# The first batch's weight conversion on fixed engine orders, one weight item per slot, low bits joined by an or on VectorE

## The chip, the cores and the metric

The kernel runs on one core of a Trainium2 chip. The metric is the device time of one execution in microseconds (us), as the median of several runs. A profile is one further execution, taken with the hardware profiler; it gives every instruction's start and length on five engines: TensorE (PE, with its weight loads as PEld), VectorE (DVE), ScalarE (ACT), GpSimd (POOL) and SyncE (SP, which here only issues the DMAs).

## The reference, cut to what matters

Three layers follow each other: an attention with 32 landmarks per head, a two-matrix layer with an exponential activation, and a maxout layer of three matrices followed by an output matrix. The weights are float64 in memory.

```
A = softmax(q @ mean(k)); Bm = softmax(mean(q) @ mean(k)); C = softmax(mean(q) @ k)
Z = start(Bm); six times: Z = 2 * Z - Z @ Bm @ Z
x = A @ Z @ C @ v                       # 8 batches of 576 tokens, 512 wide
h = x @ w_in                            # 512 -> 2048
g = where(h > 0, h, exp(min(h, 0)) - 1)
y = g @ w_out                           # 2048 -> 512
out = max(y @ w1, y @ w2, y @ w3) @ w_out2
```

## The kernel before, in words

Matrix products run as three passes in a reduced format (a high and a low part of each operand), so every operand is split: ScalarE casts the high part, and VectorE or GpSimd subtracts it from the value to get the low part (`split`, L105).

The attention of a batch ends in matrices that are folded into `w_in` (`w_step`, L645 and L650 write the folded weights `wp`). The second layer then runs in **slots**. A slot is one block of 128 hidden columns for half of a batch's tokens (288): six matmuls into `ph` (`h_mm`, L677); ScalarE's two activations of `eh` (L681, L682); VectorE's combination of them (`h_post`, L687, "eh" below); the split of the result into `gt`; and twelve matmuls `x<-gt,wo` (`x_mm`, L709), which follow three slots later (`LAG`). The first batch has slots 0 to 31, and the attention of the second batch is spread over them (`SECOND_SLOTS`): its sums stand at slots 3 to 6, its six Newton steps n0 to n5 at slots 20 to 25. A Newton step is `banks<-rr,rd` on TensorE (L237), then `rd` (L560) and `rr` (L613) on VectorE and a copy of `rr` (L611) on ScalarE. `ph` has two buffers: the matmuls of slot t need the eh of slot t-2 to be done.

In the first batch the float64 weights arrive as 32-bit words and are converted on the chip. An **item** is a block of 128 rows and 512 columns; there are 32, items 0 to 31, in the order of `PAIRS` (i: `w_in`, o: `w_out`). `widen` puts two instructions on ScalarE: a Prelu that makes a float of the upper word (L121), and a Copy that brings the three next bits of the lower word to an integer (L124). `narrow` shifts the float's bits left by three on VectorE (L130) and adds the integer on GpSimd (L133). An item of `w_out` is then split into `wo`. Items land in places that later hold other tiles; an item is loaded when the earlier holder of its place has been narrowed. By that plan items 28 and 29 follow items 24 and 25 in their places, item 30 follows item 28, and item 31 follows item 29.

Before the first slot, VectorE and ScalarE run in the written order `ORDER` ("c" narrows a pair of items, "w" widens one, the capitals are steps of the first batch's attention). From slot 0 a scheduler sets the order of all engines by priority; from slot 20 (`FIXED`) TensorE and VectorE follow the written order. ScalarE, GpSimd and SyncE follow the scheduler. Each engine works strictly through its own list, and so does SyncE with the DMAs.

Of the kernel before, what the change touches and what calls it, by code (L numbers as in the profile page):

```python
# [9 lines left out]
F32 = mybir.dt.float32  # L10
# [9 lines left out]
def landmark_attention_mlp_maxout_kernel(  # L20
# [13 lines left out]
    nc = tc.nc  # L34
# [16 lines left out]
    FPN = 512 // P  # L51
    LAG = 3

    FIXED = 20
    RA = 3

    AHEAD2 = 5
# [9 lines left out]
    PAIR_SLOTS = [0, 0, 0, 1, 1, 4, 6, 8, 9, 11, 12, 14, 15, 18, 20, 22]  # L67


    ORDER = "BBBBBBwVwBcBVVwVVwBcVVBAwBAwcBAwcBAAwBAcBAwBAAWAwcwcc"  # L70


    PAIR_LOW = [0, 0, 1, 0, 0, 1, 0, 1, 0, 0, 1, 0, 0, 0, 1, 0]
    G_LOW = [
        [0, 1, 1, 0, 0, 1, 0, 0, 1, 0, 1, 1, 0, 0, 1, 0],
        [0, 0, 0, 1, 0, 1, 1, 1, 0, 0, 0, 1, 0, 0, 0, 1],
    ]
    SOFT_SUB = [[1, 1], [1, 1]]
    SOFT_MUL = [[1, 0], [0, 0]]
    scale = 1.0 / math.sqrt(D)  # L80
# [20 lines left out]
    def split(src, hi, lo, on_dve=False):  # L101

        nc.scalar.copy(hi, src)  # L103
        eng = nc.vector if on_dve else nc.gpsimd
        eng.tensor_tensor(out=lo, in0=src, in1=hi.bitcast(F32), op=ALU.subtract)  # L105
# [6 lines left out]
            in_=src.rearrange("(f p) c -> p f c", p=P),  # L112
        )

    def widen(words, f):
# [10 lines left out]
    def narrow(words, f):  # L126


        u = f.bitcast(U32)
        nc.vector.tensor_scalar(  # L130
            out=u, in0=u, scalar1=3, scalar2=None, op0=ALU.logical_shift_left
        )
        nc.gpsimd.tensor_tensor(out=u, in0=u, in1=words[:, :, 0], op=ALU.add)  # L133
        yield

    class Conversions:
# [3 lines left out]
        def __init__(self, items, depth):  # L140
            self.items, self.depth = items, depth
            self.words, self.f = {}, {}
            self.done = -1
            self.run = self.steps()

        def fetch(self):
# [3 lines left out]
                if t is not None:  # L150
                    self.words[n] = t

        def widen(self, n):
            if n < len(self.items) and n not in self.f:
                if n not in self.words:
                    self.fetch()
                if n not in self.words:
                    return
                self.f[n] = self.items[n][1]()
                widen(self.words[n], self.f[n])  # L160

        def steps(self):
            for n in range(0, len(self.items), 2):
                both = range(n, min(n + 2, len(self.items)))
                for m in both:
                    self.widen(m)
                for _ in zip(*[narrow(self.words[m], self.f[m]) for m in both]):
                    yield
                for m in both:
                    outs = self.items[m][2]  # L170
                    if outs is not None:
                        split(self.f[m], *outs(), PAIR_LOW[n // 2])
                    self.done = m
                    self.fetch()
                for m in both:
                    if m + 2 < len(self.items) and self.items[m + 2][2] is None:
                        self.widen(m + 2)
                if self.items[n][2] is not None:
                    yield

        def upto(self, n):

            n = min(n, len(self.items))
            while self.done < n - 1:
                next(self.run)

    manual = ExitStack()
    manual.enter_context(
# [505 lines left out]
    def x_mm(b, half, f):  # L694
# [3 lines left out]
        first = f % (KF // 2) == 0 if parts else f == 0  # L698
        last = f % (KF // 2) == KF // 2 - 1 if parts else f == KF - 1
        if b == 0:  # L700
            conv.upto(index["out", f] + 1)
# [520 lines left out]

    def fits(n, p):
        if p[0] == "wp":
            return n in EARLY
        return n // 2 <= index["out", 2 * p[1]] // 2

    def plan_places():
# [47 lines left out]
    conv = Conversions(items, DEPTH)  # L1276

    def w_both(n):
        conv.upto(index["in", n * KD + KD - 1] + 1)
        w_step(0, n)  # L1280

    for g, nm in ((0, "q"), (0, "k"), (1, "q"), (1, "k")):
        load_qk(0, g, nm)
    load_v(0)
    for _ in range(NF):
        conv.fetch()
    streams = {
        "B": [
# [30 lines left out]
            streams[token].pop(0)()  # L1319
    assert not any(streams.values())  # L1320
    spare[0] = -1
    conv.upto(G)
    manual.close()


    seq = [(0, half, p * KF // 2 + f) for p in range(2) for half in range(2) for f in range(KF // 2)]
# [4 lines left out]
    def at(t, fn, *args):  # L1331
        plan[t].append((fn, args))

    load_att(1)
    load_v(1)

    def after_post(stp):


# [3 lines left out]

        return go

    for n, t in enumerate(PAIR_SLOTS):
        at(t, conv.upto, 2 * n + 2)
    for n in range(1, NCH):
        tw = (0, FPN, KF, KF + FPN)[n]
        at(tw - (2 if n == 1 else 3), w_both, n)  # L1350
    for b in range(1, B):
        t0 = (b - 1) * NSL
        if b > 1:
            at(t0 - (12 if b == 2 else 13), load_att, b)
            at(t0, load_v, b)
        for nm, stp in att_steps(b):
            if b > 1:
                at(t0 + (THIRD_SLOTS.get(nm) if b == 2 and nm in THIRD_SLOTS else STEP_SLOTS[nm]), stp)
            else:
                at(SECOND_SLOTS[nm], after_post(stp))  # L1360
        for n in range(NCH):
            at(t0 + NSL + (W_SLOTS if b > 1 else SECOND_W)[n], w_step, b, n, True)
    plain = [(i, p) for p in range(NP) for i in range(2)]
# [13 lines left out]
    manual = ExitStack()  # L1377
    for t, sl in enumerate(seq):
        if t == FIXED:
            manual.enter_context(tc.manual_schedule(engines={mybir.EngineType.PE}))  # L1380
        if t == FIXED:
            vector = ExitStack()
            vector.enter_context(tc.manual_schedule(engines={mybir.EngineType.DVE}))
        h_mm(*sl)
        late = [fn(*args) for fn, args in plan[t]]
        h_post(*sl)
        for fn in late:
            if callable(fn):
                fn()
        for parts in behind[t]:  # L1390
            next(parts, None)
        if t >= LAG:
# [132 lines left out]
```

## Time and profile before

| what | value |
|---|---|
| three runs | 1355.29, 1357.17, 1357.25 us; median 1357.17 |
| profiled execution | 1356.48 us, of which its span is 1354.7 us |
| TensorE busy | 1306.1 us (96% of the span) |
| VectorE, ScalarE, GpSimd busy | 836.6, 678.5, 690.4 us |

The 1.8 us between the span and the time of the profiled execution lie around it. A busy share is a mean over stages: in the first tenth of the span TensorE waits often, and behind that it hardly does. So the page's 96% says where little can be gained, and the stretches of the first 140 us have to be read one by one.

### The profile page before, as it was taken

The page shows a single profiled execution, that of the slowest core. Times are in us where ns is not written, and L with a number is a line of the kernel's source. Part 1 is how long each engine was busy: PE and PEld are TensorE (multiplying, and loading weights), DVE is VectorE, ACT ScalarE, POOL GpSimd, SP SyncE. Part 2 cuts the span into 40 slices and gives each one's busy share as a digit, 9 for nine tenths or more (in the row PEclk, how much of TensorE's full clock was granted, in tenths as well). Part 3 has the DMA queues.
Part 4 walks back from the last instruction along what each step waited for, and adds up shares of the span by engine and source line. Part 5 has one row for each costly group of instructions (what it writes and reads, how often), then busy time and mean ns, then how long its engine had stood idle before and what let it go on. Part 6 is the DMA issues. An engine that isn't in the chain of part 4 may idle for free.

```text
span 1354.7 us, 28499 instructions
## 1 busy us (share of the span) xinstructions
PE 1306.1 (96%) x11144; PEld 1231.5 (91%) x11144; DVE 836.6 (62%) x1601; ACT 678.5 (50%) x1576; POOL 690.4 (51%) x702
## 2 busy tenths in 40 slices
PE   4688999999999999999999999999999999999998
PEld 2477889899899998998999999999999999999998
DVE  6885745546537546455464456776677667668873
ACT  4884555656656656656566662222223223235451
POOL 2781433444435425435346456666666666665543
PEclk8588999999999999999999999999999999999999
DMA  9635104124214233142116233221322122278962
GB/s 359 224 110 167 41 19 146 64 82 149 100 41 138 104 113 97 65 166 74 66 65 189 65 120 109 86 98 55 114 86 86 56 103 97 81 286 319 310 230 78
DMA packets 102376, 168.04 MB, mean 124 GB/s; under 512 B 5985, under 2 KB 57825, under 8 KB 102241
## 3 DMA queue, kind: packets, MB, share of 16 engines
q1 hardware_dynamic: 102240, 166.22, 36.1%
q8 instruction: 87, 1.43, 0.4%
q14 instruction: 49, 0.39, 0.1%
HBM read 107.22 MB, written 58.98 MB: 123 GB/s over the span
## 4 chain that ended last, share of the span: by engine, by line
PE 89%; DMA 3%; ACT 3%; DVE 2%; issue 1%; POOL 1%; SPq 0%; DVEq 0%; ACTq 0%; POOLq 0%
PE p L1063 30%; PE x L709 28%; PE ph L677 14%; PE p L1140 10%; PE banks L237 7%; DMA words<-in_moe_w_out_dram 2%; DMA kT<-in_k_dram 1%; ACT words L124 1%; DMA raw<-w2s 0%; ACT gt L103 0%; DVE tt L765 0%; DVE eh L687 0%; DVE gt L105 0%; DMA words<-in_moe_w_in_dram 0%; ACT wp L645 0%
## 5 line engine op out<-in xcount | busy, mean ns | idle before, releaser
L709 PE MATMUL x<-gt,wo 128*128 128x288 f32 x3072 | 470.6, 303 | 4.8 <-DVE gt L105 1.4
L709 PEld LDWEIGHTS x<-gt,wo 128*128 128x128 f32 x3072 | 425.2, 190 | 45.2 <-issue 26.1
L1063 PE MATMUL p<-xo,w 128*128 128x256 f32 x3402 | 410.4, 283 | 1.0 <-DVE xo L737 1.0
L1063 PEld LDWEIGHTS p<-xo,w 128*128 128x128 f32 x3402 | 408.6, 191 | 2.8 <-ACT xo L879 1.5
L105 POOL TENSOR_TENSOR gt<-eh,gt 128x288 fp32r<-128x288 f32 x243 | 198.9, 820 | 338.2 <-ACT gt L103 306.2
L677 PE MATMUL ph<-ah,wp 128*128 128x288 f32 x1024 | 251.5, 300 | 10.0 <-DVE eh L687 4.3
L687 DVE SCALAR_TENSOR_TENSOR eh<-eh,ph 128x288 f32<-128x288 f32 x256 | 114.4, 447 | 157.3 <-ACT eh L682 113.8
L918 POOL TENSOR_TENSOR u<-s,v 128x512 f32<-128x512 f32 x99 | 132.3, 1336 | 144.9 <-DVE v L916 144.9
L677 PEld LDWEIGHTS ph<-ah,wp 128*128 128x128 f32 x1024 | 182.1, 192 | 17.6 <-DVE eh L687 7.7
L103 ACT CAST gt<-eh 128x288 fp32r<-128x288 f32 x256 | 110.4, 432 | 108.3 <-DVE eh L687 108.1
L681 ACT ACTIVATE eh<-ph 128x288 f32<-128x288 f32 x256 | 104.5, 410 | 116.4 <-PE ph L677 91.2
L907 ACT COPY s<-p 128x512 f32<-128x512 f32 x99 | 57.9, 585 | 198.9 <-PE p L1063 172.2
L677 PE MATMUL ph<-al,wp 128*128 128x288 f32 x512 | 153.7, 300 | 2.1 <-POOL al L105 2.1
L1140 PE MATMUL p<-wo,ho 128*128 128x256 f32 x1134 | 133.2, 280 | 0.0
L1140 PEld LDWEIGHTS p<-wo,ho 128*128 128x128 f32 x1134 | 133.1, 188 | 0.0
L682 ACT ACTIVATE eh<-eh 128x288 f32<-128x288 f32 x256 | 113.8, 446 | 5.1
L677 PEld LDWEIGHTS ph<-al,wp 128*128 128x128 f32 x512 | 98.3, 192 | 2.5 <-POOL al L105 2.5
L931 DVE TENSOR_TENSOR t<-p,u 128x512 f32<-128x512 f32 x81 | 55.8, 689 | 72.1 <-POOL u L918 69.5
L1130 DVE TENSOR_TENSOR ho<-hf,ho 128x768 fp32r<-128x768 f32 x54 | 73.6, 1390 | 13.6 <-ACT ho L1128 12.8
L1070 DVE TENSOR_TENSOR t<-t 128x1024 f32<-128x1024 f32 x54 | 70.6, 1307 | 6.4 <-POOL t L921 0.4
L921 POOL TENSOR_TENSOR t<-u,s 128x256 f32<-128x256 f32 x81 | 67.1, 829 | 5.4
L133 POOL TENSOR_TENSOR wf<-wf,words 128x512 uint32<-128x512 uint32 x40 | 54.9, 1381 | 28.9 <-DVE wf L130 22.9
(164 smaller groups left out, 1391.8 us busy)
## 6 DMA issues: line engine op xcount, KB each, us to landing
hf<-hs SPq DMA_DIRECT2D x63, 384.0 KB, 4.5
hs<-t SPq DMA_DIRECT2D x27, 512.0 KB, 3.0
xs<-xo SPq DMA_DIRECT2D x36, 288.0 KB, 3.3
hs<-s SPq DMA_DIRECT2D x27, 384.0 KB, 3.4
qT<-in_q_dram SPq DMA_DIRECT2D x16, 576.0 KB, 6.3
kT<-in_k_dram SPq DMA_DIRECT2D x16, 576.0 KB, 7.5
words<-in_moe_w_dram SPq DMA_DIRECT2D x9, 1024.0 KB, 5.1
xf<-xs SPq DMA_DIRECT2D x9, 1024.0 KB, 5.0
```

Source lines behind the costliest of these rows:

```text
L103: nc.scalar.copy(hi, src)
L105: eng.tensor_tensor(out=lo, in0=src, in1=hi.bitcast(F32), op=ALU.subtract)
L237: ins = fn(*args, **kw)
L677: nc.tensor.matmul(ph[:, :HF], a, c, start=(g == 0 and j == 0), stop=(g == 1 and j == 2))
L681: nc.scalar.activation(e, ph[:, :HF], AF.Relu, scale=-1.0)
L682: nc.scalar.activation(e, e, AF.Exp, scale=-1.0)
L687: state["post"] = nc.vector.scalar_tensor_tensor(out=e, in0=e, scalar=1.0, in1=ph[:, :HF], op0=ALU.subtract, op1=ALU.max)
L709: nc.tensor.matmul(xacc[ec][:, :HF], a, gt[:, c], start=(first and j == 0), stop=(last and j == 2),)
L918: nc.gpsimd.tensor_tensor(out=u57, in0=s57, in1=v.unsqueeze(1).to_broadcast([P, 2, 256]), op=ALU.add)
L1063: nc.tensor.matmul(dst, l, r, start=(c == 0 and j == 0), stop=(c == 1 and j == 2))
L1130: eng.tensor_tensor(out=lo, in0=v, in1=hi.bitcast(F32), op=ALU.subtract)
L1140: nc.tensor.matmul(dst, l, r, start=(c == 0 and n == 0), stop=(c == NP - 1 and n == 2))
```

## The change

From slot 0 VectorE and TensorE, and to slot 26 also ScalarE, follow the written order; GpSimd and SyncE stay with the scheduler. `ORDER` is rewritten: ten items (`FRONT`) are widened before slot 0. Then slot t widens item 10+t, narrows item 9+t and splits item 8+t. Items 0 to 9 keep ScalarE's Copy (with a factor that can't round up to 8), and VectorE shifts and ors in one instruction. From item 10 on ScalarE's Copy is gone: VectorE multiplies the lower word and cuts it at 7 (one instruction), and shifts and ors in a second. GpSimd's addition is gone from the first batch. All low parts of `wo` are now subtracted on GpSimd; those of `gt` alternate, even columns on GpSimd and odd ones on VectorE.

```
-    FIXED = 20
+    FIXED_ACT = 27
-    DEPTH = 8
-    EARLY = range(8, 26)
-    G = 4
+    DEPTH = 12
+    EARLY = {2: range(8, 22), 3: range(8, 26)}
+    FRONT = 10
-    ORDER = "BBBBBBwVwBcBVVwVVwBcVVBAwBAwcBAwcBAAwBAcBAwBAAWAwcwcc"
+    ORDER = "BBBBwwBBVBBVVVVwwBVVBAcwBAwBcAwBAAwBAAwBAwBAWAccc"
-    G_LOW = [
-        [0, 1, 1, 0, 0, 1, 0, 0, 1, 0, 1, 1, 0, 0, 1, 0],
...
+    G_LOW = [[0, 1] * 8, [0, 1] * 8]
...
-        nc.scalar.activation(words[:, :, 0], words[:, :, 0], AF.Copy, scale=2.0**-29)
...
+        if form != BITS_V:
+            scale = 2.0**-29 if form == ADD else 2.0**-29 * (7.49 / 8)
+            nc.scalar.activation(words[:, :, 0], words[:, :, 0], AF.Copy, scale=scale)
...
+        if form == BITS_V:
+            nc.vector.tensor_scalar(
+                out=low, in0=low, scalar1=2.0**-29, scalar2=7.0, op0=ALU.mult, op1=ALU.min
+            )
...
+            nc.vector.scalar_tensor_tensor(
+                out=u,
+                in0=u,
+                scalar=3,
+                in1=low,
+                op0=ALU.logical_shift_left,
+                op1=ALU.bitwise_or,
+            )
...
-            lambda: r_s.tile([P, 512], F32, tag=f"wf{f % 2}", name="wf"),
+            lambda: r_s.tile([P, 512], F32, tag=f"wf{f % 3}", name="wf"),
...
-    for n, t in enumerate(PAIR_SLOTS):
-        at(t, conv.upto, 2 * n + 2)
...
+        if t == 0:
+            scalar.close()
+            scalar = ExitStack()
             manual.enter_context(tc.manual_schedule(engines={mybir.EngineType.PE}))
             vector.enter_context(tc.manual_schedule(engines={mybir.EngineType.DVE}))
+            scalar.enter_context(tc.manual_schedule(engines={mybir.EngineType.Activation}))
+        if t == FIXED_ACT:
+            scalar.close()
         h_mm(*sl)
+        if t < len(items):
+            stage(conv.widen, FRONT + t, BITS_V)
...
+        if t < len(items):
+            stage(conv.narrow, FRONT + t - 1, BITS_V)
+            stage(conv.cast, FRONT + t - 2)
+            stage(conv.low, FRONT + t - 2)
```

Three places of the new order matter below. The first is VectorE ahead of the first Newton step of batch 0. Before:

```order
L514 TENSOR_REDUCE st<-bb 128x4
L130 TENSOR_SCALAR w_in_sb<-w_in_sb 128x512 x2
L527 STREAM_TRANSPOSE sT<-st 128x32
L530 TENSOR_REDUCE tn<-sT 128x1
L531 COPY mb<-tn 128x32
```

Now (the line numbers are those of the changed file, 17 higher there):

```order
L531 TENSOR_REDUCE st<-bb 128x4
L544 STREAM_TRANSPOSE sT<-st 128x32
L547 TENSOR_REDUCE tn<-sT 128x1
L548 COPY mb<-tn 128x32
L549 STREAM_TRANSPOSE sT<-mb 128x32
```

The two shifts no longer stand in this chain; their successors (L135) stand behind the first Newton step.

The second place is ScalarE around the Newton steps n0 and n1 of the second batch (slots 20 and 21). Before:

```order
L681 ACTIVATE eh<-ph 128x288
L682 ACTIVATE eh<-eh 128x288
L611 COPY rr_97<-banks 128x2x32
L103 CAST gt<-eh 128x288
L421 ACTIVATE x<-x 128x576
L681 ACTIVATE eh<-ph 128x288
L682 ACTIVATE eh<-eh 128x288
L611 COPY rr_96<-banks 128x2x32
```

Now, with the widening of items 30 and 31 (L113 wf<-words):

```order
L698 ACTIVATE eh<-ph 128x288
L699 ACTIVATE eh<-eh 128x288
L113 ACTIVATE wf<-words 128x512
L628 COPY rr_97<-banks 128x2x32
L438 ACTIVATE x<-x 128x576
L96 CAST gt<-eh 128x288
L180 CAST wo<-wf 128x512
L698 ACTIVATE eh<-ph 128x288
L699 ACTIVATE eh<-eh 128x288
L113 ACTIVATE wf<-words 128x512
L628 COPY rr_96<-banks 128x2x32
```

A widening now stands directly ahead of each of the two copies. VectorE's `rr` waits for that copy, and TensorE's next Newton step for that `rr`.

The third place is SyncE with the last loads. Before:

```order
L110 DMA words<-in_moe_w_out_dram 128x1024 x2
L738 DMA xs<-xo 128x2x288 x2
L725 DMA xo<-xs 128x2x288 x2
L269 DMA v<-in_v_dram 128x4x512
L272 DMA v<-in_v_dram 64x512
L263 DMA qT<-in_q_dram 128x2x576
```

Now the single L103 rows are items 30 and 31:

```order
L103 DMA words<-in_moe_w_out_dram 128x1024 x2
L286 DMA v<-in_v_dram 128x4x512
L289 DMA v<-in_v_dram 64x512
L280 DMA qT<-in_q_dram 128x2x576
L280 DMA kT<-in_k_dram 128x2x576
L755 DMA xs<-xo 128x2x288 x2
L280 DMA qT<-in_q_dram 128x2x576
L280 DMA kT<-in_k_dram 128x2x576
L103 DMA words<-in_moe_w_out_dram 128x1024
L742 DMA xo<-xs 128x2x288 x2
L103 DMA words<-in_moe_w_out_dram 128x1024
```

The last two items are now loaded behind the third batch's v, q and k.

## Rows read from the trace of the kernel before

**Rows 1.** Busy time by stretch: us, then each engine's busy time, granted clock, DMA.

```profile
68.00:102.00 34.00, 28.88 (x214) 25.30 (x213) 28.29 (x57) 28.48 (x68) 28.91 (x24) 0.90 0.32 108
136.00:170.00 34.00, 34.00 (x277) 30.26 (x276) 26.29 (x49) 20.34 (x52) 16.18 (x17) 1.00 0.12 38
...
340.00:1000.00 660.00, 658.39 (x5642) 622.66 (x5641) 379.69 (x779) 345.84 (x851) 338.42 (x369) 1.00 0.30 98
```

**Rows 2.** TensorE in order of time, 128 to 138 us: start, us, instruction, idle before.

```profile
129.51 3.23 PE L709 MATMUL x<-gt,wo 128*128 128x288 f32 x12
...
133.86 0.60 PE L237 MATMUL banks<-rr,rd 128*128 128x128 f32 x4
134.22 1.82 PE L709 MATMUL x<-gt,wo 128*128 128x288 f32 x12
...
136.68 0.60 PE L237 MATMUL banks<-rr,rd 128*128 128x128 f32 x4
```

**Rows 3.** VectorE in order of time, 16 to 25 us.

```profile
16.41 0.74 DVE L130 TENSOR_SCALAR w_in_sb<-w_in_sb 128x512 uint32<-128x512 uint32 x1
...
18.79 0.20 DVE L527 STREAM_TRANSPOSE sT<-st 128x32 f32<-128x32 f32 x1
...
19.25 1.09 DVE L531 COPY mb<-tn 128x32 f32<-128x32 f32 x1
...
24.46 0.47 DVE L489 TENSOR_SCALAR rr<-ptv,rs 128x64 f32<-128x64 f32 x2
```

**Rows 4.** VectorE in order of time, 40 to 58 us.

```profile
40.66 0.23 DVE L613 TENSOR_TENSOR rr<-pn,rr 128x64 f32<-128x64 f32 x1 [0.20 <-PE pn L237]
...
41.57 0.99 DVE L426 TENSOR_SCALAR t<-t 128x18 f32<-128x18 f32 x1
...
49.35 2.87 DVE L130 TENSOR_SCALAR w_in_sb<-w_in_sb 128x512 uint32<-128x512 uint32 x3
...
56.90 0.80 DVE L687 SCALAR_TENSOR_TENSOR eh<-eh,ph 128x288 f32<-128x288 f32 x2
```

**Rows 5.** VectorE's groups by shape: count, busy us, mean ns, idle before.

```profile
L687 DVE SCALAR_TENSOR_TENSOR eh<-eh,ph 128x288 f32<-128x288 f32 x256 | 114.4, 447 | 157.3 <-ACT eh L682 113.8 <-POOL gt L105 43.2 <-issue 0.2
...
L650 DVE TENSOR_TENSOR wp<-banks,wp 128x512 fp32r<-128x512 f32 x62 | 39.9, 685 | 36.6 <-ACT wp L645 33.2 <-PE ph L677 1.9 <-PE x L709 1.5
...
L281 DVE TENSOR_REDUCE kT<-kT 128x64 f32<-128x1152 f32 x16 | 21.5, 1345 | 0.3 <-DMA kT<-in_k_dram 0.2
...
L105 DVE TENSOR_TENSOR gt<-eh,gt 128x288 fp32r<-128x288 f32 x13 | 10.0, 773 | 3.9 <-ACT gt L103 3.9
```

**Rows 6.** VectorE in order of time: single instructions from 60 to 119 us.

```profile
63.80 0.68 DVE L105 TENSOR_TENSOR wo<-wf,wo 128x512 fp32r<-128x512 f32 x1
...
64.73 0.42 DVE L130 TENSOR_SCALAR w_in_sb<-w_in_sb 128x512 uint32<-128x512 uint32 x1
...
78.28 1.57 DVE L105 TENSOR_TENSOR gt<-eh,gt 128x288 fp32r<-128x288 f32 x1
...
104.78 0.44 DVE L105 TENSOR_TENSOR gt<-eh,gt 128x288 fp32r<-128x288 f32 x1
...
117.22 0.45 DVE L687 SCALAR_TENSOR_TENSOR eh<-eh,ph 128x288 f32<-128x288 f32 x1
...
118.17 0.46 DVE L105 TENSOR_TENSOR gt<-eh,gt 128x288 fp32r<-128x288 f32 x1 [0.50 <-ACT gt L103]
```

**Rows 7.** GpSimd in order of time, at 78 us.

```profile
78.04 1.50 POOL L133 TENSOR_TENSOR w_in_sb<-w_in_sb,words 128x512 uint32<-128x512 uint32 x1
```

**Rows 8.** The chain that ended last, in order of time: start, us, what.

```profile
54.34 3.98 DMA words<-in_moe_w_out_dram
...
154.40 0.80 PE ph L677 x6
155.19 1.61 PE x L709 x12
```

**Rows 9.** ScalarE's groups by shape: the widening's Prelu.

```profile
L121 ACT ACTIVATE wf<-words 128x512 f32<-128x512 f32 x40 | 27.0, 674 | 12.7 <-DMA words<-in_moe_w_dram 10.8 <-DMA words<-in_moe_w_out_dram 1.2 <-POOL wo L105 0.6
```

More of the change, by code (lines that the diff above doesn't have):

```diff
@@ L113, in load_words, with widen @@
         )
-    def widen(words, f):
+    ADD, BITS, BITS_V = range(3)
+    def widen(words, f, form=ADD):
         nc.scalar.activation(
@@ L142, in __init__ @@
             self.words, self.f = {}, {}
-            self.done = -1
+            self.done = self.ready = -1
+            self.outs = {}
             self.run = self.steps()
@@ L151, in fetch, with widen @@
                     self.words[n] = t
[L153 to L160, printed above, removed]
+        def widen(self, n, form=BITS):
+            while n not in self.words:
+                before = len(self.words)
+                self.fetch()
+                assert len(self.words) > before
+            self.f[n] = self.items[n][1]()
+            widen(self.words[n], self.f[n], form)
@@ new lines, in narrow, with cast, low @@
+        def narrow(self, n, form=BITS):
+            for _ in narrow(self.words[n], self.f[n], form):
+                pass
+            self.done = n
+            self.fetch()
+        def cast(self, n):
+            if self.items[n][2] is not None:
+                self.outs[n] = self.items[n][2]()
+                nc.scalar.copy(self.outs[n][0], self.f[n])
+        def low(self, n):
+            if self.items[n][2] is not None:
+                hi, lo = self.outs[n]
+                nc.gpsimd.tensor_tensor(
+                    out=lo, in0=self.f[n], in1=hi.bitcast(F32), op=ALU.subtract
+                )
+            self.ready = n
@@ L162, in steps @@
         def steps(self):
-            for n in range(0, len(self.items), 2):
-                both = range(n, min(n + 2, len(self.items)))
+            for n in range(0, FRONT, 2):
+                both = range(n, n + 2)
                 for m in both:
-                    self.widen(m)
-                for _ in zip(*[narrow(self.words[m], self.f[m]) for m in both]):
-                    yield
[L169 to L185, printed above, removed]
+                    self.narrow(m)
+                yield
+                if self.items[n][2] is not None:
+                    for m in both:
+                        self.cast(m)
+                    for m in both:
+                        self.low(m)
+                    yield
+                self.ready = n + 1
     manual = ExitStack()
@@ L700, in x_mm @@
         if b == 0:
-            conv.upto(index["out", f] + 1)
+            assert conv.ready >= index["out", f]
         if first:
@@ L1278, in w_both @@
     def w_both(n):
-        conv.upto(index["in", n * KD + KD - 1] + 1)
-        w_step(0, n)
+        assert conv.done >= index["in", n * KD + KD - 1]
+        return w_step(0, n, True)
     for g, nm in ((0, "q"), (0, "k"), (1, "q"), (1, "k")):
         load_qk(0, g, nm)
-    load_v(0)
-    for _ in range(NF):
+    for n in range(NF):
+        if n == 3:
+            load_v(0)
         conv.fetch()
@@ L1344, in after_post @@
         return go
-    for n, t in enumerate(PAIR_SLOTS):
-        at(t, conv.upto, 2 * n + 2)
-    for n in range(1, NCH):
-        tw = (0, FPN, KF, KF + FPN)[n]
-        at(tw - (2 if n == 1 else 3), w_both, n)
+    at(0, load_att, 1)
+    at(2, load_v, 1)
     for b in range(1, B):
@@ L1362, in landmark_attention_mlp_maxout_kernel @@
             at(t0 + NSL + (W_SLOTS if b > 1 else SECOND_W)[n], w_step, b, n, True)
+    for n in range(1, NCH):
+        tw = (0, FPN, KF, KF + FPN)[n]
+        at(tw - (2 if n == 1 else 3), w_both, n)
     plain = [(i, p) for p in range(NP) for i in range(2)]
@@ L1391, in landmark_attention_mlp_maxout_kernel @@
             next(parts, None)
+        if t == 0:
+            next(conv.run, None)
+        if t < len(items):
+            stage(conv.narrow, FRONT + t - 1, BITS_V)
+            stage(conv.cast, FRONT + t - 2)
+            stage(conv.low, FRONT + t - 2)
         if t >= LAG:
```

33 lines of the change are left out of this document (14 added, 19 removed).

## The prediction

> **What bounds the kernel now.** I read the stretches first, then TensorE's timeline at the end of the first batch, VectorE's timeline ahead of the first slot, and VectorE's groups. From 68 to 102 us TensorE works 28.88 of 34 us at a granted clock of 0.90, while VectorE, ScalarE and GpSimd are each busy for over 28 us; from 136 us on TensorE is busy all the time, and so it stays [rows 1]. A gain must therefore arise before about 136 us. As a marker I take the Newton step n2 of the second batch, in slot 22: in both kernels TensorE follows the written order there, with the same work before and after it. It starts at 136.68 [rows 2]. What follows takes 1354.7 - 136.7 = 1218.0 us, and 1.8 us lie around the span. So the question is when n2 starts in the changed kernel.
>
> **Part 1, up to the first eh (slot 0).** In the chain ahead of the first Newton step the two shifts take 16.41 to 18.79 = 2.4 us, most of it a wait; the copy L531 takes 1.09 beside a GpSimd addition, where its neighbour takes 0.20, so 0.9 goes; a second pair of shifts (0.7) stands directly before L489 [rows 3]. L489 could start at 24.46 - 4.0 = 20.5, but it needs `ptv`, which then ends at about 21.2 by the lengths it has now. I take 21.4. The Newton steps of the first batch run from 24.46 to 40.89 [rows 3, 4]. Walking through the new list with today's durations, each step is 0.85 us of `rd` and `rr` plus the longer of TensorE's 1.2 and what VectorE has in between (an or pair of 1.3, a reduction of 0.7): 14.2 us, to 35.6. From there to the first eh it is 56.90 - 40.89 = 16.0 us now; two small scalar steps of 0.99, which need 0.2 when GpSimd is idle, and eight shifts at 2.87 / 3 = 0.96 us [rows 4] stand in it. Afterwards only four ors (2.5 us) do, and the folded weights (42.07 to 47.7 today) come with the Newton chain. The walk gives `wp` done at 40.9, the second half's transpose at 42.2, the four ors at 44.6, the first eh at E0 = 45.0: 11.9 us earlier than 56.90. I hold this to be good to 2 us either way.
>
> **Part 2, slots 0 to 18 on VectorE's list.** The new list is strict, so I add it up, with lengths start to start (0.07 less than a row's).
> - 19 eh at 0.37 (0.447 long [rows 5]): 7.0.
> - Nine odd slots: the subtraction (0.37) follows eh directly and must wait for ScalarE's cast; from eh to it 0.95 us pass (117.22 to 118.17 [rows 6]), so 0.58 of waiting: 9 x 0.95 = 8.6.
> - Items 8 and 9 in slot 0: 1.2. Then 18 items, each a multiplication and an or. The trace has neither. A two-input instruction of 512 columns takes 0.68; a one-input one took 0.42, but on contiguous words, and here they are strided [rows 6]. Bounds: 1.05 and 1.31 an item. I take 1.1, near the shift, which is the same kind of instruction: 19.8.
> - The sums of the second batch, four at 1.27 (1.345 long) [rows 5]: 5.1; three pairs of folded weights at 1.2 (0.685 each) [rows 5]: 3.6; the other second-batch steps of these slots by their present lengths: 11.2, and 0.95 for two exponentials on ScalarE ahead of slot 9's cast.
>
> That is 57.5. In slots 6, 14 and 16 TensorE's own slot is longer: a slot is 0.80 + 1.61 = 2.41 us there [rows 8]; 2.1 more. Then GpSimd: VectorE's subtraction at 78.28 took 1.57 where a free one takes 0.44, and beside it GpSimd's addition took 1.50 [rows 6, 7]; the mean over 13 was 0.773, so 0.33 of waiting [rows 5], with GpSimd busy 28.91 of 34 us [rows 1]. Its work here is about half of that share, and two to three instructions a slot are exposed: 0.4 a slot (0 if it never meets, 2.5 x 1.1 = 2.8 if it always does), 7.6. So eh of slot 19 starts at E19 = 45.0 + 67.2 = 112.2, and the step n1 could start 4.2 later, at 116.4 (now 133.86 [rows 2]).
>
> That is 3.5 us a slot, hardly shorter than today. ScalarE (some 2.2 us a slot without the Copy) and GpSimd (1.7) stay below it, so the saved Copy and addition are hidden. Part 2 gains only by having fewer hold-ups around slots 20 and 21.
>
> **Part 3, the loads of items 30 and 31.** I expect this to eat most of it. Item 30 goes to the place of item 28, which is narrowed in slot 19, at E19 + 0.95 + 0.37 + 1.1 + 0.1 = E19 + 2.5. ScalarE wants to widen item 30 right after the second activation of slot 20, and the copy for n0 stands behind it; VectorE's `rr` waits for that copy, ahead of the eh of slot 20, and TensorE's n1 waits for `rr`. A load of this size took 3.98 us on the chain [rows 8], and four q and k loads and two stores go ahead of it: I take 4.7, landing at E19 + 7.2. With 0.67 for the widening [rows 9], 0.2 for the copy, 0.3 for `rr` and 0.1 for hand-overs n1 starts at E19 + 8.5, and eh of slot 20 at E19 + 9.2. Item 29 is narrowed 1.5 later, item 31 loaded in 4.0, and the same 1.3 follow: n2 at E19 + 16.0 = 128.2. Without the loads it would be 2.9 behind n1, at 119.3; they cost 8.9. The bounds are 8 (two bare loads) and 15 (both 3 us later). There is little other work to hide it, since TensorE itself stands at n1 and n2.
>
> **Part 4, the clock.** After today's waits the twelve matmuls at 129.51 took 3.23 us against 1.82 at 134.22 [rows 2], at the lower of the two levels, and the six after them 0.5 more: 1.9 us. After the stall at n2 I charge this once; bounds 0 and 3.
>
> **Sum.** n2 128.2 against 136.7: -8.5; clock +1.9: -6.6. Span 1348.1, with 1.8 around it 1349.9. The profiled execution (1356.48) stands 0.7 below the median of the runs; I predict 1350.
>
> **Rivals.**
> 1. TensorE sets the pace, because VectorE's list overlaps better than I add it. A slot is then 2.41 plus some 0.35 of second-batch steps, 19 slots 53 us, E19 near 99, n2 at 115, the time about 1338. For it: from 102 us on VectorE idles today. Against it: the list of 57.5 us without any waiting on GpSimd.
> 2. Slower: VectorE's strict list keeps meeting GpSimd's subtractions. The or and the odd subtraction read two operands in SBUF like the one at 78.28, and an eh behind a held or holds TensorE two slots on. If the wait is 1.2 us a slot instead of 0.4, 15 us are lost: 1365. It decides from 0.75 a slot. Against it: GpSimd loses its additions.
> 3. No difference: the loads land 3 us later each, behind q and k: 1356. For it: the q and k loads are issued just ahead.
>
> On rival 2 the Trainium skill has a rule (SBUF — State Buffer, section on the two separate sides): VectorE and GpSimd share a port pair as an exclusive lock held for a whole instruction, and a VectorE instruction with two SBUF inputs needs it. By it the or is exposed, although the nearest instruction of its kind, eh with one input in PSUM, keeps 0.447 over 256; by that row alone the lock term would be 4.6 and the time 1347, by the rule it is the 7.6 of the sum. Rows 6 and 7 agree with the rule for the subtraction; no row shows it for an or.
>
> **How the numbers follow.** A measurement can tell 0.2%, 2.7 us. Forecast: 0.50, with its own range 1343 to 1354.4; rival 1: 0.20; rival 3: 0.15; rival 2: 0.15. So faster 0.70, within 0.2% 0.15, slower 0.15. Items at 1.31 add 3.8 us, the GpSimd term reaches from -7.6 to well over +15, the loads from -1 to +6, the prologue 2 either way. For 8 in 10 I take 1336 to 1360, which leaves out most of rival 2 and the far end of rival 1.
>
> **What would show it.** Right: first eh near 45 us; ors of 0.68 alone and longer beside GpSimd; eh 3 to 4 us apart in slots 2 to 18; ScalarE idle before the widening in slots 20 and 21 with a DMA of `words` as releaser; TensorE waiting at `banks<-rr,rd` for `rr`, some 4 us each; n2 near 128. Wrong: no wait at n1 and n2; a first eh behind 48; slots at 2.8 us (rival 1) or above 4.2 (rival 2).

## The result, and the profile after

The changed kernel takes 1366.23 us (median, 1365.79 to 1367.25) where the kernel before took 1357.21 in the same session: a ratio of 1.0071, 95% interval 1.0053 to 1.0088. It is slower by 9.0 us; forecast were 7 us faster, with 1336 to 1360 as the range. The profiled execution has a span of 1364.5 us, 9.8 more than before. Marks that both traces have divide this difference; n0 is a good one, since TensorE has done 738 matmuls ahead of it in both:

| stretch | before, us | after, us | after less before | forecast for after |
|---|---|---|---|---|
| start to the first eh | 56.90 | 44.68 | -12.2 | 45.0 |
| first eh to the Newton step n0 | 71.7 | 76.5 | +4.8 | |
| n0 to n2 | 8.0 | 19.8 | +11.8 | |
| n2 to the end | 1218.0 | 1223.5 | +5.5 | 1219.9 |
| eh of slot 0 to eh of slot 19 | 60.3 | 75.0 | | 67.2 |
| eh of slot 19 to n2 | 19.5 | 21.4 | | 16.0 |

(Before, eh of slot 0 starts at 56.90 [rows 4], where one row holds the eh of slots 0 and 1, eh of slot 19 at 117.22 [rows 6], n0 at 128.64 and n2 at 136.68 [rows 2]. After, eh of slots 0, 18 and 19, n0 and n2 start at 44.68, 116.68, 119.64, 121.19 and 141.02.) The first stretch came as forecast. Of its gain 7.5 us are left at n0; the two steps behind n0 lose 11.8 us, and what follows n2 another 5.5. The last two rows are for the terms of the forecast alone: up to eh of slot 19 the two kernels have not done the same work on TensorE, since the new order puts more of the second batch's attention and of the folded weights ahead of it.

TensorE's matmuls ahead of n0, by stretch (us, then each engine's busy time, granted clock, DMA), before and after:

```profile
0.00:128.60 128.60, 86.92 (x738) 67.19 (x738) 94.55 (x211) 84.91 (x193) 64.55 (x59) 0.81 0.59 208
```

```profile
0.00:121.15 121.15, 83.74 (x738) 66.12 (x739) 91.24 (x216) 71.77 (x165) 36.00 (x36) 0.86 0.58 206
```

The stretches, by the view that answers to [rows 1]: us, then each engine's busy time, with the granted clock near the end. After:

```profile
68.00:102.00 34.00, 25.69 (x226) 22.50 (x227) 25.62 (x68) 22.07 (x51) 11.64 (x10) 0.91 0.15 49
136.00:170.00 34.00, 28.31 (x200) 24.62 (x200) 22.48 (x46) 17.20 (x46) 14.09 (x14) 0.89 0.17 51
340.00:1000.00 660.00, 658.60 (x5643) 621.67 (x5644) 377.90 (x777) 352.38 (x868) 337.89 (x370) 1.00 0.29 96
```

From 68 to 102 us GpSimd is busy 11.64 us where it was 28.91, ScalarE 22.07 where it was 28.48. But VectorE, which now has more to do in a slot, is busy 25.62 where it was 28.29, and TensorE 25.69 where it was 28.88. No engine is full, so they wait for each other. From 340 to 1000 us next to nothing differs.

TensorE in order of time, the stretch of [rows 2] (start, us, instruction, idle before and its releaser); n0 before, then n0 to n5 after:

```profile
128.64 1.22 PE L237 MATMUL banks<-rr,rd 128*128 128x128 f32 x4 [1.03 <-DVE x L405]
```

```profile
121.19 0.60 PE L254 MATMUL banks<-rr,rd 128*128 128x128 f32 x4
...
132.81 1.23 PE L254 MATMUL banks<-rr,rd 128*128 128x128 f32 x4 [8.64 <-DVE rr L630]
133.68 3.12 PE L726 MATMUL x<-gt,wo 128*128 128x288 f32 x12
...
141.02 1.22 PE L254 MATMUL banks<-rr,rd 128*128 128x128 f32 x4 [3.42 <-DVE rr L630]
141.90 3.23 PE L726 MATMUL x<-gt,wo 128*128 128x288 f32 x12
...
147.37 0.71 PE L254 MATMUL banks<-rr,rd 128*128 128x128 f32 x4 [0.81 <-DVE rr L630]
147.84 1.84 PE L726 MATMUL x<-gt,wo 128*128 128x288 f32 x12
...
150.73 0.71 PE L254 MATMUL banks<-rr,rd 128*128 128x128 f32 x4 [0.28 <-DVE rr L630]
...
154.41 0.71 PE L254 MATMUL banks<-rr,rd 128*128 128x128 f32 x4 [0.58 <-DVE rr L630]
```

n0 stands 7.5 us ahead of the kernel before, n1 waits 8.64 us, n2 3.42, both for `rr`. The matmuls behind each of the two waits run at the lower of the two clock levels: they take 3.12 and 3.23 us against 1.84, with a granted clock of 0.51 from 132.8 to 136.6 us and 0.50 from 141.0 to 146.5. The chain of waits (start, us, what) tells what `rr` waited for:

```profile
122.40 1.55 SPq L280
...
124.06 7.53 DMA words<-in_moe_w_out_dram
...
131.66 0.66 ACT wf L113
132.32 0.11 ACT rr L628
...
132.46 0.29 DVE rr L630
...
135.04 0.70 DVE wf L135
...
135.80 4.00 DMA words<-in_moe_w_out_dram
...
139.88 0.66 ACT wf L113
140.54 0.11 ACT rr L628
...
140.68 0.29 DVE rr L630
```

This is the forecast chain, link by link: the load of item 30, its widening, the copy of `rr` behind it on ScalarE, `rr`, TensorE; then the narrowing of item 29, the load of item 31, and the same again. The second load takes the 4.0 us of a bare one [rows 8]; the first takes 7.53, with q and k just ahead of it in the queue. That q and k are what it waits for was not tested by itself.

For slots 0 to 18 the list of waits of VectorE, 45 to 120 us, says more than any timeline (what waited, for what: us in total, times, longest):

```profile
DVE gt L98 <- ACT gt L96: 8.8, 9, 2.3
DVE eh L704 <- ACT eh L699: 3.7, 2, 3.0
DVE rr L506 <- PE banks L254: 1.1, 1, 1.1
DVE mx L349 <- ACT e L356: 1.0, 2, 0.5
DVE x L422 <- PE banks L254: 0.9, 1, 0.9
DVE et L490 <- PE banks L254: 0.5, 1, 0.5
DVE wp L667 <- ACT wp L662: 0.5, 1, 0.5
```

These waits sum to 16.5 us. In the kernel before, over slots 0 to 19 (56.8 to 117.3 us), the list sums to 12.4 us, and the wait for the cast of `gt` is this line of it:

```profile
DVE gt L105 <- ACT gt L103: 1.9, 3, 0.7
```

There the scheduler had put other work behind eh, and the low part of `gt` later. In the written order the low part of `gt` stands directly behind eh in every odd slot, so VectorE stands still while ScalarE gets to its cast, 8.8 us in nine times. In all, VectorE waits some 4 us more than before; from the first eh to n0 it is also busy 57.5 us instead of 52.3, as it has the new instructions.

The new instructions, by VectorE's groups from 44.6 to 119.6 us (count, busy us, mean ns, idle before):

```profile
L135 DVE SCALAR_TENSOR_TENSOR w_in_sb<-w_in_sb,words 128x512 uint32<-128x512 uint32 x10 | 9.4, 950 | 0.3
L126 DVE TENSOR_SCALAR words<-words 128x512 uint32<-128x512 uint32 x18 | 8.8, 491 | 0.0
L135 DVE SCALAR_TENSOR_TENSOR wf<-wf,words 128x512 uint32<-128x512 uint32 x10 | 8.8, 882 | 0.6
```

and by single instructions, VectorE first, then GpSimd at the same time:

```profile
52.39 1.53 DVE L126 TENSOR_SCALAR words<-words 128x512 uint32<-128x512 uint32 x1
53.96 0.69 DVE L135 SCALAR_TENSOR_TENSOR wf<-wf,words 128x512 uint32<-128x512 uint32 x1
...
57.15 0.42 DVE L126 TENSOR_SCALAR words<-words 128x512 uint32<-128x512 uint32 x1
57.61 1.67 DVE L135 SCALAR_TENSOR_TENSOR wf<-wf,words 128x512 uint32<-128x512 uint32 x1
```

```profile
52.33 1.30 POOL L185 TENSOR_TENSOR wo<-wf,wo 128x512 fp32r<-128x512 f32 x1
57.35 1.38 POOL L185 TENSOR_TENSOR wo<-wf,wo 128x512 fp32r<-128x512 f32 x1 [3.72 <-ACT wo L180]
```

An or takes 0.69 alone and 1.67 beside GpSimd's subtraction, a multiplication 0.42 and 1.53. Twenty ors cost 18.2 us instead of 13.8 (20 x 0.69) and 18 multiplications 8.8 instead of 7.6: 5.6 us of holding in all.

### The profile page after: what moved, and what is told of

Same layout as the page of the kernel before. It is cut to its first block, busy times and chain, and to the rows that moved or that the text cites. A ratio compares the mean times of both kernels' runs of the same rounds, so it can differ in the third digit from the quotient of the medians.

```text
span 1364.5 us, 28425 instructions
## 1 busy us (share of the span) xinstructions
PE 1305.9 (96%) x11144; PEld 1232.1 (90%) x11144; DVE 839.9 (62%) x1616; ACT 668.8 (49%) x1554; POOL 661.5 (48%) x677
## 4 chain that ended last, share of the span: by engine, by line
PE 87%; DVE 5%; ACT 3%; DMA 2%; issue 2%; POOL 1%; SPq 0%; DVEq 0%; POOLq 0%; ACTq 0%
PE p L1080 30%; PE x L726 27%; PE ph L694 13%; PE p L1157 10%; PE banks L254 6%; DMA words<-in_moe_w_out_dram 1%; DVE w_in_sb L135 1%; ACT gt L96 1%; DMA kT<-in_k_dram 0%; DVE kT L298 0%; DVE wp L667 0%; DVE eh L704 0%; DVE words L126 0%; ACT wp L662 0%; DVE wf L135 0%
## 5 line engine op out<-in xcount | busy, mean ns | idle before, releaser
L938 POOL TENSOR_TENSOR t<-u,s 128x256 f32<-128x256 f32 x81 | 67.2, 829 | 5.4
L1145 ACT CAST ho<-hf 128x768 fp32r<-128x768 f32 x63 | 51.0, 836 | 36.7 <-DMA hf<-hs 17.4
```

## The experiments

Two theories stood against each other at first. **A**: the late loads of items 30 and 31 cost the time, as the chain above shows. **B, C, D**: the strict lists, VectorE and GpSimd holding each other, or the or itself. Each ratio is to the kernel before, run on the same chip, with its 95% interval. Differences from the changed kernel or from another experiment compare medians; the kernel before had medians of 1356.2 to 1357.2 us beside them, so such a difference is good to no better than 1 us.

**Other places for the last items (e1).** Item 30 could not be loaded before item 28 was narrowed, one slot ahead of its own widening. This edit gives items 26 to 31 other places:

```
         if p[0] == "wp":
             return n in EARLY[p[1]]
+        if n in {5: (28, 29), 6: (26, 27), 7: (26, 27, 28, 29)}.get(p[1], ()):
+            return False
```

> The changed kernel with other places for items 26 to 31 alone (26, 27 follow 16, 17; 28, 29 follow 14, 15; 30, 31 follow 24, 25), so that items 30 and 31 can be loaded once items 24 and 25 are narrowed, five slots ahead of their widening; VectorE's, ScalarE's and TensorE's orders stay. Theory A (the late loads of items 30 and 31 hold ScalarE's list, the copy of rr behind it and so TensorE): eh of slot 19 stays near 119.6 us, TensorE's waits of 8.6 and 3.4 us at n1 and n2 go, n2 starts near 127 instead of 141.0, the matmuls behind it run at full clock, and the time is 1347 to 1351 us. Rival B (the strict lists themselves, with VectorE meeting GpSimd, pace slots 20 to 25 at some 4 us each): n2 near 132 to 134, further waits at n3 to n5, the time 1355 to 1360. Rival C (GpSimd and VectorE holding each other everywhere, loads hidden anyway): 1362 to 1366.

Measured: 1357.65 us, ratio 1.0004 (0.9995 to 1.0012); 8.6 us less than the changed kernel. TensorE at n1 to n3:

```profile
124.87 0.71 PE L254 MATMUL banks<-rr,rd 128*128 128x128 f32 x4
...
131.01 0.71 PE L254 MATMUL banks<-rr,rd 128*128 128x128 f32 x4 [3.03 <-DVE rr L630]
...
137.36 0.71 PE L254 MATMUL banks<-rr,rd 128*128 128x128 f32 x4 [1.73 <-DVE rr L630]
```

n1's wait is gone, n2 comes 10 us earlier. eh of slot 18 stays at 116.81. So the loads were worth 9 us, as far as they could be seen; but A expected 15 to 19, since n2 and n3 wait again, now 3.03 and 1.73. The time is one that rival B named (1355 to 1360), and n2 comes just ahead of its 132 to 134, so e1 alone does not decide between the two. ScalarE's list, in order of time, names the new wait:

```profile
126.74 0.69 ACT L438 ACTIVATE x<-x 128x576 f32<-128x576 f32 x1 [2.25 <-POOL x L430]
127.33 0.42 ACT L96 CAST gt<-eh 128x288 fp32r<-128x288 f32 x1
...
129.87 0.66 ACT L113 ACTIVATE wf<-words 128x512 f32<-128x512 f32 x1 [0.65 <-DMA kT<-in_k_dram]
130.44 0.20 ACT L628 COPY rr<-banks 128x64 f32<-128x64 f32 x1
```

An exponential waits 2.25 us for GpSimd, a cast, two activations and a widening follow, and only then the next copy of `rr`.

**Items 30 and 31 widened two slots later (e2).** Short form of the edit: `s = ci - FRONT + (2 if ci >= 30 else 0)` in place of `ci - FRONT`, with the widening behind the cast of `gt` for these two.

> The changed kernel with the places and loads as they are, but items 30 and 31 are widened two slots later (22 and 23), behind the copy of rr in ScalarE's list, and narrowed and split two slots later too. Theory A: n1 and n2 no longer wait for the loads; item 30 lands near 131 us, slot 22's widening waits some 2 to 3 us and holds ScalarE's next activations that long; n2 near 127, the time 1349 to 1354 us. Rival B: 1356 to 1361. Rival C: 1362 to 1366.

Measured: 1358.16 us, ratio 1.0011 (1.0002 to 1.0020). n1 at 123.95 and n2 at 128.62, as A says; but the weights of these items came late in turn: TensorE waits 2.48 and 1.14 us for `wo` in slot 25. So A's time, 1349 to 1354, was missed by 4 us, and the time is again one that B named. It is a second way to the same 8 us, with a new price.

**The old addition in the new orders (e4).**

```
-            stage(conv.widen, FRONT + t, BITS_V)
+            stage(conv.widen, FRONT + t, ADD)
...
-            stage(conv.narrow, FRONT + t - 1, BITS_V)
+            stage(conv.narrow, FRONT + t - 1, ADD)
```

> The changed kernel with the old form for items 10 to 31 (ScalarE's Copy, VectorE's shift, GpSimd's addition instead of VectorE's multiplication and or); places, slots and orders otherwise as in the changed kernel. Theory A: slots 0 to 18 are paced by waits among the engines as much as by VectorE's list, so VectorE's 0.6 us less a slot is offset by GpSimd's 1.4 more; the late loads stay, as narrowing now ends on GpSimd: eh of slot 19 at 115 to 123 us, the time 1362 to 1375 us. Rival D (the or and the multiplication on VectorE's list are what made the kernel slower): eh of slot 19 some 11 us earlier and the time near 1355 us.

Measured: 1370.19 us, ratio 1.0093 (1.0077 to 1.0109). eh of slot 18 starts at 117.18 (116.68 in the changed kernel), although VectorE is busy 8.4 us less in slots 0 to 18 (45.8 instead of 54.2); its waits for the cast of `gt` grow to 11.7 us. D is refuted as stated: the old form is no faster in these orders. The edit also gives ScalarE its Copy back ahead of the cast (busy 54.9 us instead of 44.6) and GpSimd its addition, so it does not show what VectorE's instructions cost by themselves.

**The or alone, in the old orders (e6).** ScalarE's Copy stays, VectorE shifts and ors in one instruction, GpSimd's addition goes.

> The kernel before with one edit: the low bits come by ScalarE's Copy and one shift-and-or on VectorE instead of VectorE's shift and GpSimd's addition; all orders, pairs and slots of the kernel before. Theory A (the or itself is not what made it slower): GpSimd is relieved of 28 us, the first eh comes some 2 to 5 us earlier, the time is 1350 to 1358 us. Rival D: VectorE's ors beside GpSimd's subtractions slow the slots, the time is 1360 or more.

Measured: 1358.08 us, ratio 1.0006 (0.9997 to 1.0015): no difference. The forecast that the first eh comes earlier was wrong (65.26 against 56.90), and by slot 24 TensorE was within 3 us of the kernel before (its matmuls `ph` start at 144.32 against 141.52). So in the old orders this or changes nothing, and in the new orders the old form is no faster (e4): the orders decide. The form with the multiplication was not run in the old orders.

**The softmax exponentials one slot later (e7).**

```
-        if b:
+        if b > 1:
             soft_ax(b, g)
...
+    for g in range(2):
+        at(21 + g, after_post(lambda g=g: soft_ax(1, g)))
```

> e1 with one more edit: ScalarE's softmax exponentials of the second batch (x, behind GpSimd's subtraction) are issued one slot later, in slots 21 and 22 instead of 20 and 21. In e1 each waits 2.25 us for GpSimd with the cast of gt, the next slot's activations, a widening and the copy of rr behind it. Theory A2 (these two waits took the place of the loads): TensorE's waits of 3.03 and 1.73 us at n2 and n3 go, n2 starts near 128 instead of 131.0, n3 near 131 instead of 137.4, and the time is 1350 to 1353 us. Rival E (another wait in the same strict lists, such as VectorE's or of 1.6 us beside GpSimd or the widening that waits for a buffer, ends nearly as late): 1354 to 1358 us.

Measured: 1355.93 us, ratio 0.9997 (0.9988 to 1.0006), at best 2 us less than e1. n2 still waits 3.38 us, since the cast of `wo` in the same list now waits 1.94 us for VectorE's or. Rival E holds: in this list another wait ends nearly as late.

**VectorE's low part of gt behind the or (e8).** To e1 it adds:

```
+            state["low"] = lambda: nc.vector.tensor_tensor(
+                out=gt[:, 1], in0=e, in1=gt[:, 0].bitcast(F32), op=ALU.subtract
+            )
...
             stage(conv.low, FRONT + t - 2)
+        if "low" in state:
+            state.pop("low")()
```

> e1 with one more edit: in odd slots VectorE's low part of gt stands behind the multiplication and the or of the slot instead of directly behind eh, so that the two fill the time in which ScalarE casts gt. Theory F (the slots are long because VectorE's strict list waits for ScalarE: 8.8 us in front of the low parts of gt in slots 0 to 18): eh of slot 18 at 107 to 111 us instead of 116.8, the time 1348 to 1353 us. Rival G (a loop over ScalarE and TensorE paces the slots, and VectorE's wait only moves to the next eh): eh of slot 18 at 114 to 117 us and the time 1355 to 1358.

Measured: 1347.11 us, ratio 0.9931 (0.9917 to 0.9945): 10 us less than e1. eh of slot 18 starts at 107.89. VectorE's waits from 45 to 110 us:

```profile
DVE wp L667 <- ACT wp L662: 2.8, 2, 2.0
...
DVE gt L710 <- ACT gt L709: 0.7, 1, 0.7
```

8.8 us of waiting for the cast have become 0.7, and the slots are shorter by 8.9. F holds (the time is just under its 1348 to 1353), G falls.

**Both (e9).**

> e1 with the edits of e7 and e8 together. Theories A2 and F: the two gains lie one behind the other and add: 1341 to 1349 us. Rivals E and G: 1352 to 1358 us.

Measured: 1347.01 us, ratio 0.9931 (0.9918 to 0.9945). That is inside the range that was named for two gains, but by e8's gain alone: the edit of e7 adds nothing to e8.

**ScalarE's order left to the scheduler (e10).** The edit is `FIXED_ACT = 0` on top of e1.

> e1 with ScalarE's order left to the scheduler from slot 0 on instead of the written order up to slot 26; VectorE and TensorE stay in written order. Theory H (ScalarE's strict list, one widening ahead of every cast, is what makes slots 0 to 18 take 4.0 us each against 3.35 in the kernel before): eh of slot 18 five or more us earlier than 116.8 and the time 1347 to 1353. Rival (VectorE's strict list does it, whatever ScalarE's order is): eh of slot 18 within 2 us of 116.8, the time 1354 to 1360.

Measured: 1360.81 us, ratio 1.0034 (1.0021 to 1.0047). eh of slot 18 starts at 122.09, 5.3 us later than in e1; 3.0 of them arise before the first eh (47.53 against 44.55). From 47 to 122 us ScalarE's widenings wait 6.6 us for loads of `words`, which they don't in e1, and VectorE still waits 9.4 us for the casts. H is refuted as stated, and the rival's bounds were missed too; this kernel's written order for ScalarE is better than none. (The 3.35 us in the expectation take the eh of slot 19, at 117.22, for that of slot 18. In the kernel before, the eh of slot 18 starts at 115.55, so slots 0 to 18 took 3.26 us each.)

**The places of a pair exchanged (e11).** `for hl in (0, 1)` in place of `(1, 0)`, on top of e9.

> e9 with one more edit: in each pair of places the first item lies in the tile of the high parts and the second in that of the low parts (in e1 to e10 it is the other way round). In e7 and e9 ScalarE's cast of wo of item 28 writes the tile in which the words of item 29 lie, and so waits for VectorE's narrowing of item 29 (1.94 us in e7), with the next slot's activations, a widening and the copy of rr behind it. Theory K (this wait is what kept n2 late after the softmax exponentials were moved): TensorE's wait of 3.38 us at n2 falls under 1 us and the time is 1342 to 1345 us, 2 to 5 below e9. Rival L (the or of the slot, the widening or the loads of q and k hold the copy of rr as long): within 1 us of e9's 1347.

Measured: 1347.05 us, ratio 0.9932 (0.9917 to 0.9947). K's wait is gone, but n2 waits 2.81 us: the widening ahead of the copy of `rr` now waits 2.03 us for a buffer that GpSimd frees (`wf` has three). Rival L holds.

**The edit of e8 without the other places (e12).**

> The changed kernel (places and loads as they are) with only the edit of e8: VectorE's low part of gt stands behind the slot's multiplication and or. If the loss in slots 0 to 18 and the loss at the late loads are independent, eh of slot 18 comes at 107 to 109 us, the waits at n1 and n2 stay at 8 to 12 us together, and the time is 1355 to 1358 us, some 9 to 10 below the changed kernel's 1366. If the earlier slots only run into the loads sooner (q, k and the last items set the time at which items 30 and 31 land), the waits at n1 and n2 grow and the time is 1360 to 1366 us.

Measured: 1357.42 us, ratio 1.0008 (0.9998 to 1.0018), 8.8 us less than the changed kernel. eh of slot 18 at 107.48, the waits at n1 and n2 8.95 and 3.16. So the two losses are independent to within 2 us: e1 takes back 8.6, e12 8.8, and e8, which has both edits, 19.1.

**The low parts of wp behind the or (e13).** In slots 2, 13 and 17, on top of e11: `for fn in late: ... fn()` moved behind `stage(conv.narrow, ...)`.

> e11 with one more edit: in slots 2, 13 and 17 VectorE's two low parts of the folded weights wp stand behind the slot's multiplication and or instead of ahead of them (in e8 VectorE waits 2.00 us for ScalarE's cast of wp in slot 17 and 0.82 in slot 2). If VectorE's list still paces these slots: 1 to 3 us below e11. Rival: TensorE waits for wp or for the banks instead: within 1 us of e11, or above it.

Measured: 1344.50 us, ratio 0.9923 (0.9902 to 0.9944): 2.5 below e11, though their intervals overlap.

**All low parts of gt on GpSimd (e14).** `G_LOW = [[0] * 16, [0] * 16]`, on top of e1.

> e1 with all low parts of gt in the first batch on GpSimd, so that VectorE has none of them and waits for no cast of gt. Theory F (what e8 gains is the wait for ScalarE's cast): eh of slot 18 at 106 to 111 us and the time 1347 to 1352 us, like e8's. Rival M (e8 gains because its ors no longer run beside GpSimd's subtractions): GpSimd has 16 more of them, VectorE's ors and multiplications meet them more often, eh of slot 18 stays at 113 to 118 us and the time at 1354 to 1359 us.

Measured: 1343.80 us, ratio 0.9912 (0.9896 to 0.9927). eh of slot 18 at 106.89, the time 3 us below the range of F. M, and with it the rival that VectorE and GpSimd holding each other is the loss, is refuted: the two meet more often, as the groups show (44.6 to 107.5 us),

```profile
L135 DVE SCALAR_TENSOR_TENSOR w_in_sb<-w_in_sb,words 128x512 uint32<-128x512 uint32 x11 | 11.2, 1026 | 0.3
L126 DVE TENSOR_SCALAR words<-words 128x512 uint32<-128x512 uint32 x18 | 10.3, 574 | 0.0
...
L135 DVE SCALAR_TENSOR_TENSOR wf<-wf,words 128x512 uint32<-128x512 uint32 x9 | 7.4, 822 | 0.5
```

7.5 us of holding (18.6 - 13.8 for twenty ors, 10.3 - 7.6) where the changed kernel has 5.6, and yet the slots are 10 us shorter: what went is VectorE's wait for a cast, and with it 2.4 us of VectorE's own work (busy 51.8 us instead of 54.2).

**The widening behind the copy of rr, loads as they are (e16).** The changed kernel with:

```
-        if t < len(items):
+        if t < 20:
             stage(conv.widen, FRONT + t, BITS_V)
...
         h_post(*sl)
+        if 20 <= t < len(items):
+            stage(conv.widen, FRONT + t, BITS_V)
```

> The changed kernel with one edit: in slots 20 and 21 ScalarE widens items 30 and 31 behind the copy of rr and the cast of gt instead of ahead of them; places and loads as in the changed kernel. Theory N: TensorE's n1 has no wait (near 124.4 us instead of 132.8); the next slot's activations still stand behind the widening of item 30, which lands near 131.7, so the copy for n2 comes near 133.6 and n2 near 134 instead of 141.0: 1357 to 1361 us. Rival P (the loads hold the slots by another way, as by the words' places or the buffers of wf, whatever the copy's place): n1 or n2 wait as long as before and the time is 1363 to 1367 us.

Measured: 1358.45 us, ratio 1.0020 (1.0010 to 1.0030), 7.8 less than the changed kernel, with the loads as late as before:

```profile
124.81 0.71 PE L254 MATMUL banks<-rr,rd 128*128 128x128 f32 x4 [0.45 <-DVE rr L630]
133.53 1.22 PE L254 MATMUL banks<-rr,rd 128*128 128x128 f32 x4 [5.62 <-DVE rr L630]
```

N expected n1 near 124.4 and n2 near 134. What n2 still waits for is the copy behind the activations of slot 21, and these stand behind the widening of item 30, which waits 3.40 us for its load. The load costs time only through what stands behind the widening.

**Everything together (e15, and e17 with the edit of e13).** e14 with the edits of e7, e11 and e16.

> e14 (other places, all low parts of gt on GpSimd) with the edits of e7 and e11, and with the widening of items 30 and 31 behind the copy of rr and the cast of gt in slots 20 and 21. Theory N (n2 is late because the copy of rr stands behind a widening, whatever that waits for): TensorE's waits at n1 to n3 (0.2, 3.07 and 1.55 us in e14) shrink to under 1 us together, n2 starts near 118 us, the time is 1338 to 1341 us. Rival O (VectorE's rd behind the or beside GpSimd, or the next activations behind the widening, end as late): 1342 to 1346 us.

> e15 with the edit of e13 (VectorE's low parts of wp behind the slot's multiplication and or in slots 2, 13 and 17). If VectorE's waits for ScalarE still cost time in slots 0 to 18 (2.00 us in slot 17 of e14): 1 to 3 us below e15. Rival: within 1 us of e15.

Measured: e15 1338.64 us, ratio 0.9874 (0.9861 to 0.9888); e17 1338.20, ratio 0.9871 (0.9856 to 0.9886), no difference between them, as the rival of e17 said. TensorE at n1 to n3 in e15:

```profile
114.17 0.61 PE L254 MATMUL banks<-rr,rd 128*128 128x128 f32 x4
...
117.41 0.71 PE L254 MATMUL banks<-rr,rd 128*128 128x128 f32 x4 [0.25 <-DVE rr L630]
...
121.70 0.71 PE L254 MATMUL banks<-rr,rd 128*128 128x128 f32 x4 [1.18 <-DVE rr L630]
```

The waits sum to 1.4 us, where N expected under 1; n2 and the time came as it said. In e7 and e11, which lack the edit of e16, n2 still waits 3.38 and 2.81 us; with it, 0.25. What that edit does without those of e7 and e11 was not run with these places. Both kernels beat the one before by 1.3% and the changed one by 28 us. By the marks of the first table, e15's gain on the kernel before is 11.7 us ahead of the first eh (45.25), 5.6 from there to n0 (66.1) and 2.0 from n0 to n2 (6.1); 2.2 us are lost behind n2.

## Why the prediction was wrong, by its own steps

The forecast span was 1348.1 us; the measured one is 16.4 longer. The steps that failed are VectorE's waiting in part 2 (7.8 us) and the length of the loads in part 3 (5.4), and part 4 put the clock and the waits behind n2 too low (3.6). By the terms:

- **Part 1, the first eh at 45.0: right in the sum** (44.68), with some luck. The chain was faster than walked (the second half's transpose is done at 40.99 instead of 42.2), and the four ors took 3.7 us instead of 2.5, the last two of them 2.51 beside two GpSimd subtractions. Two readings were off and change little: of the 2.4 us of the first shifts 1.2 were a wait, not most, and of the two steps of 0.99 the second took 0.69.
- **Part 2, 67.2 us for slots 0 to 18 and one eh: the step that failed, by 7.8.** The list itself was well priced: an item's multiplication and or take 0.46 + 0.61 = 1.07 us start to start (1.1 was taken), and the holding beside GpSimd 5.6 us (7.6). What failed is the sentence that VectorE's list could be added up with 0.58 of waiting in an odd slot, and that ScalarE and GpSimd "stay below it". The list of waits sums to 16.5 us, where the working had 8.25 (5.2 for the nine casts, 0.95 for the exponentials, 2.1 for TensorE). With 2.0 less of holding this leaves 1.5 of the 7.8, which were not followed up. An average busy share below VectorE's does not mean that ScalarE is there in time: its own strict list has a widening ahead of each cast, and that widening at times waits for GpSimd (2.9 us in three times, 45 to 120 us). e8, e12 and e14 show it; each takes away VectorE's wait for the cast, and eh of slot 18 comes 9 to 10 us earlier.
- **Also in part 2: a comparison that was wrong, though no term hung on it.** It said "hardly shorter than today" of 3.5 us a slot. Up to eh of slot 19 a slot took 60.3 / 19 = 3.17 us before, so the forecast slots were longer than those of the kernel before.
- **Part 3, the loads: the right chain, undersized by 5.4.** From eh of slot 19 to n2 it was 21.4 us, forecast 16.0. Item 30's load took 7.53 (4.7 was taken, bare 3.98), SyncE was busy with k for 0.4, item 28 was narrowed at 4.0 instead of 2.5 (the or beside GpSimd, and the cast late), and 0.7 came at item 31. By the working's own count, in which n2 would stand 7.1 behind eh of slot 19 without the loads, they cost 14.3, near the stated bound of 15. What the text did not see is that the loads hide others: without them, exponential, cast and buffer hold the same copy of `rr` for 3 us (e1, e7, e11), and n2 stands 10.6 behind eh of slot 19 in e1. The cause is the copy's place in ScalarE's list, as e16 and e15 show.
- **Part 4, the clock and what follows n2: 5.5 instead of 1.9.** From n2 to n3, without n3's wait, 147.37 - 0.81 - 141.02 = 5.5 us pass at the lower level, against 139.50 - 136.68 = 2.8 before: the clock costs 2.7, where 1.9 was charged. The new waits at n3 to n5 (0.81, 0.28, 0.58) add 1.7, which the text had left out. The remaining 1.1, most of it behind n5, was not followed up.

**The rivals.** Rival 2 named 1365 us, within 1.3 of the result, and its mechanism is refuted: the holding beside GpSimd cost 5.6 us where the rival needed 23 (1.2 in each of 19 slots), and e14, with more of it, is faster. A rival's number can be met for another reason. Rival 3 (later loads) happened in addition: item 30's load took 3.5 us more than a bare one. Rival 1 (TensorE paces, near 1338) is another number met for another reason: e15 measures its time, but not by its mechanism. Slots 0 to 18 take 3.4 us each there, not 2.8, and eh of slot 19 comes at 109.8, not near 99; n2 comes at 117.4 because only 7.6 us lie between the two.

On the holding itself, the row shows an or of 0.69 alone and 1.67 beside a subtraction of 1.38. The Trainium skill's rule (SBUF — State Buffer, section on the two separate sides), by which a VectorE instruction with two SBUF inputs is blocked until a GpSimd instruction that reads SBUF and started first has finished, agrees with it. The trace also shows the multiplication, with a single input, at 0.42 alone and 1.53 beside a subtraction of 1.30. The Trainium skill (VectorE: DVE Perf Modes, section on the mode 2×_2P) says that an instruction with one source, from SBUF to SBUF, can use both read ports, and it says (SBUF — State Buffer, section on who interferes with whom) that it then contends with GpSimd. Both agree with this row, though no run shows which mode the instruction ran in. No term of the sum hung on the second rule.

## What to carry to other kernels

When a written order replaces a scheduler's, a list's own lengths are not its price: read each engine's list of waits, and put between an instruction and its consumer on another engine whatever work is ready. An instruction that can wait for a load, a buffer or another engine should stand behind the short copy that a critical chain needs, not ahead of it; removing what it waits for only brings up the next wait. Compare stretch by stretch with the old trace before counting a gain ahead of it, and between marks that have the same work ahead of them in both kernels, as n0 has here and eh of slot 19 has not.

## What the runs showed of the hardware that was not expected

The granted clock from 40 to 60 us was 0.50 in the kernel before, 0.72 in the changed one and 1.00 in e6, with TensorE busy 12.14, 14.89 and 10.54 us of the 20 in that order; e6 has 56 matmuls there, the kernel before 62. So TensorE was granted the lower level throughout in one kernel and the higher one in another that was busy for less of the stretch; the work is not the same instruction by instruction, and why is open. A DMA of 512 KB took 4.00 us alone and 7.53 behind q and k, while the DMA engines were busy for 0.95 of the time (121 to 132 us). In a row of waits, a releaser "DMA kT" stands ahead of a widening that reads no kT (0.65 us in e1); which DMA it waited for the trace does not say.
